# Twelve filler matmuls and a written order in a fused attention and MLP kernel

## The chip, the core and the metric

One core of one Trainium2 chip runs the whole program. The metric is the device time of one execution in microseconds (us); the time of a version is the median over its runs, and lower is better.

## What is computed

Eight batches of attention with eight heads, 576 queries and keys of 64 elements, and 16 beacon keys that every query sees; then a two-layer MLP with a squared ReLU over all 8 x 576 = 4608 tokens.

```python
k_all = np.concatenate([beacon_k, k], axis=2)      # (8, 8, 16 + 576, 64)
v_all = np.concatenate([beacon_v, v], axis=2)
scores = scale * np.matmul(q, k_all.transpose(0, 1, 3, 2))
scores = np.where(causal, -1000000000.0, scores)
a = np.exp(scores - scores.max(-1, keepdims=True))
a /= a.sum(-1, keepdims=True) + 1e-09
attn = np.matmul(a, v_all)                         # -> x: (4608, 512)
...
r = np.maximum(x @ w_in, 0.0)                      # w_in (512, 2048)
out = (r * r) @ w_out                              # w_out (2048, 512)
```

## The kernel before

**Steps.** The kernel is built from 1,521 named steps. A step is an `Op` (L93): a name, the engines that may run it, what it depends on, the buffers that it takes and gives back, and a function that emits its instructions. Names carry the batch or chunk: `ld2k4` loads the fifth slice of batch 2's k (L440), `cast2k4` makes it bf16 on GpSimd (L396), `tr2k` transposes the batch's k by DMA (L472), `qk8.2` computes scores (L687), `exp8.2...` exponentiates them on ScalarE (L789; L711 in batch 0), `mask` applies the causal mask (L811), `av8.0.0` multiplies by v on TensorE (L833), `norm` divides by the row sums (L851, L853), `xt` transposes the result by DMA (L885) into the ring buffer `xT`. Chunks of 512 tokens then go through `s1` (x @ w_in, L1146), `relu` and `sq`, `s2` (the second product, L1197 in the first two chunks, L1260 after them), `ev` (PSUM to `osb`) and `st` (the store to HBM, L1185, L1315).

**Batch 0 and 1** take another way: `fldk`, `fldq`, `sld` load q and k (L586, L515), and TensorE transposes them (`tp`, L547 and L550) into PSUM; `eq` and `ek` copy the result to `qT` and `kT`. In batch 0 the four pairs of heads are computed in two phases (`qk3.0.0`, then `qk3.1.0` and so on). TensorE also transposes the attention output of batches 0 to 2 (`xtp`, L902).

**Queues.** The loads of batches 0 and 1 and both weight matrices are issued by GpSimd (`sld`, `ld0v`, `win`, `sld1`, `ld1v`, `wout`, in this order). All else that is loaded, every DMA transpose and every store but one is issued by SyncE, each in its place in one queue: `ld2k0`, the first of batch 2, waits for the last quarter of `w_out` (`sync`, L1357). Slices pass through six staging buffers `stg`.

**Order.** `Order.run` (L144) is a list planner that runs when the program is built. It keeps a clock of its own with a duration for each step, and whenever an engine is free it starts the ready step of the lowest priority number; `NUDGE` (L17) shifts 275 priorities and `HOME` (L77) binds steps to engines. The steps are emitted in the order of their planned starts. PSUM is handed out as two double banks (`strips`) and four single banks (`ps`); a bank goes back to the end of its list at the moment when the planner's clock sees the step done that reads it last (L181 to L186).

Around the start, TensorE's first work is the transpose `tp0.0.0q`, which waits for `fcq0`, a cast on ScalarE of the first loaded slice of q.

Of the kernel before, what the change touches and what calls it, by code (L numbers as in the profile page):

```python
# [10 lines left out]
BF16 = mybir.dt.bfloat16  # L11
# [5 lines left out]
NUDGE = {  # L17
    "fldk0": 658.071, "fldk1": 538.534, "fcq3": -23.8, "bkl0": 22.188, "ek0.0.0": -25.42, "tp0.0.1k": -476.9,
    "eq0.0.3": -51.138, "tp0.1.0k": -975.238, "eq0.1.0": -201.003, "tp0.1.1k": 92.697, "ek0.1.1": -17.465,
    "tp0.1.2k": -1278.23, "ek0.1.3": -50.758, "eq0.1.3": 210.345, "qk2.1.0": -1322.85, "qk3.1.0": -1576.95,  # L20
    "qk3.1.2": 98696.4, "xte0.0.1": 72.837, "xte0.0.2": 202.007, "xtp0.1.1": 1543.7, "xtp0.1.3": 299.523,
    "tp1.0.0k": -36.734, "tp1.0.2q": 99521.3, "tp1.0.3k": 99518.5, "mask4.0.2": -52.183, "exp5.7.-1.1.0": -4.503,
    "exp5.7.0.0.0": 466.023, "qk6.10": 99505.4, "exp6.10.-1.0.0": 90.776, "exp6.10.-1.1.0": 79.415,
    "exp6.10.1.0.1": 147.224, "exp7.13.-1.1.0": -161.243, "xte1.0.2": 65.923, "s1.0.0.0": -97989.7,
    "relu0.0.0": 0.295, "s1.0.1.0": -98820.7, "relu0.0.1": 179.265, "sq0.0.1": 54.421, "s1.0.2.0": -300.425,
    "s1.0.3.0": -98822.7, "s1.0.2.1": -118.835, "s1.0.3.1": 8.01, "relu0.3.1": -97.929, "sq0.1.1": -91.845,
    "s1.0.8.1": -99593.7, "sq0.4.1": -12.447, "s1.0.11.0": -100291.234, "relu0.10.1": -97.474,
    "s1.0.11.1": -100375.057, "sq0.5.1": -107.919, "sq0.2.0": -108.607, "s1.0.4.1": 45.995, "s1.0.5.1": -257.73,
    "s1.0.6.0": -12.465, "s1.0.7.0": 328.542, "s1.0.6.1": 126.896, "relu0.6.1": 736.189, "s1.0.12.0": -261.69,
    "s1.0.12.1": -260.74, "s1.0.13.1": -30.691, "s1.0.15.0": 310.934, "sq0.7.0": 214.775, "s1.0.14.1": -78.077,  # L30
    "s1.0.15.1": -476.91, "relu0.15.1": 417.533, "s2.0.1.0": 341.138, "s2.0.2.1": 207.549, "s2.0.3.2": 112.672,
    "s1.1.0.0": 108.494, "s1.1.8.0": 54.353, "s1.1.10.0": 53.3, "s1.1.11.0": 94.01, "s1.1.7.0": 463.778,
    "relu1.7.0": 14.618, "s1.1.12.0": 963.577, "ev1.0": -9.252, "st2": 304.472, "s2.1.2.0": 154.455,
    "s2.1.3.2": 256.085, "ev1.3": -16.524, "av8.0.0": 100447.244, "exp9.7.0.0.0": 31.254, "qk10.10": -1291.46,
    "exp10.10.-1.1.0": -214.735, "relu2.0.0": -393.283, "s1.2.1.0": 160.98, "s1.2.8.0": 1108.37, "s1.2.9.0": 1253.63,
    "s1.2.10.0": -101520.500, "relu2.10.0": -9.869, "s1.2.11.0": -99.215, "s1.2.5.0": -101090.066,
    "s1.2.6.0": -100738.217, "s1.2.7.0": -100723.318, "sq2.3.0": -5.02, "s1.2.12.0": -100712.441,
    "s1.2.13.0": -102656.973, "s1.2.14.0": -102349.519, "s1.2.15.0": 239.8, "sum2.4.0": 1465.92, "sum2.3.0": 1466.01,
    "sum2.3.1": 1606.78, "s2.2.1.1": 823.901, "s2.2.5.0": 76.569, "st5": 565.41, "qk12.5": -1133.88,
    "exp12.5.0.0.0": 293.348, "qk13.8": -830.36, "exp14.11.-1.0.0": -65.743, "exp14.11.-1.1.0": 564.369,  # L40
    "mask14.0.1": -1428.96, "norm15.0.0": 218.979, "xt3.1": 8.184, "xt3.3": 202.161, "s1.3.2.0": 16.151,
    "relu3.2.0": 24.317, "s1.3.10.0": -27.427, "s1.3.11.0": 295.381, "s1.3.5.0": 22.355, "sq3.2.0": -7.233,
    "s1.3.7.0": 5.062, "sq3.3.0": 38.235, "s1.3.15.0": 105.093, "sum3.4.0": 2134.7, "s2.3.2.1": -101383.148,
    "s2.3.6.0": -101211.097, "ev3.u2.None": 150.941, "s2.3.4.1": -101244.799, "st7": 333.885, "qk16.2": 101478.821,
    "exp16.5.0.0.0": 448.591, "av18.0.0": 101516.209, "av18.0.1": 101561.876, "av19.0.0": 101281.365, "xt4.0": 2.246,
    "xt4.3": 248.657, "s1.4.0.0": 1038.21, "s1.4.1.0": -912.296, "s1.4.2.0": 57.023, "sq4.1.0": 11.294,
    "s1.4.8.0": 22.523, "s1.4.9.0": -907.487, "s1.4.11.0": 97.493, "sq4.5.0": -5.964, "s1.4.4.0": -101628.248,
    "s1.4.5.0": 124.134, "s1.4.6.0": 259.779, "relu4.7.0": -11.452, "s1.4.12.0": -102373.044, "relu4.12.0": -342.413,
    "sq4.6.0": 2063.88, "s1.4.14.0": -102369.452, "s2.4.2.0": -102160.747, "s2.4.6.0": 1139.26, "s2.4.5.0": 1742.19,
    "ld5k0": -144.81, "ld5k1": 108.018, "ld5v3": -131.083, "exp20.2.1.0.0": 2412.05, "qk20.5": -126.513,  # L50
    "av20.0.1": 601.406, "exp21.8.0.0.0": -36.383, "exp22.11.0.0.0": -3.784, "xt5.2": 229.366, "xt5.3": 136.903,
    "xt5.4": 110.02, "s1.5.0.0": 35.934, "s1.5.1.0": 178.108, "s1.5.2.0": -1138.86, "relu5.2.0": 7.05,
    "s1.5.3.0": 135.127, "sq5.1.0": -15.732, "s1.5.9.0": -1205.53, "s1.5.11.0": -647.533, "s1.5.4.0": 4.138,
    "s1.5.6.0": 127.935, "s1.5.7.0": -102665.329, "relu5.7.0": -5.3, "s1.5.13.0": 1028.46, "sq5.6.0": 95.713,
    "s1.5.15.0": 365.66, "s2.5.6.1": -102540.099, "s2.5.4.1": -102308.653, "ld6q2": 240.402, "tr6k": -117.387,
    "ld6v0": -220.207, "ld6v1": -231.765, "ld6v2": 23.728, "exp24.2.1.0.0": 20.556, "qk24.5": -215.651,
    "exp24.5.-1.0.0": -166.742, "av24.0.0": 102704.684, "av25.0.0": 102763.978, "exp26.11.-1.0.0": 299.914,
    "xt6.1": 154.988, "xt6.3": 265.679, "s1.6.0.0": 1862.08, "s1.6.1.0": 1656.3, "s1.6.2.0": 868.136,
    "relu6.2.0": -22.081, "s1.6.8.0": 10.058, "relu6.8.0": 18.852, "s1.6.9.0": -103734.110, "sq6.4.0": -332.773,
    "s1.6.10.0": -103829.821, "relu6.10.0": 326.623, "s1.6.11.0": -97.927, "relu6.11.0": 31.773, "relu6.4.0": 42.741,  # L60
    "s1.6.6.0": -103698.974, "s1.6.7.0": -581.885, "s1.6.12.0": 60.655, "s1.6.13.0": -41.185, "relu6.13.0": -218.8,
    "relu6.15.0": -324.763, "sum6.4.1": 177.924, "s2.6.7.0": 1165.61, "ev6.u3.None": -28.927, "s2.6.4.1": 2162.64,
    "ld7q4": 33.222, "ld7v2": 112.962, "ld7v4": 152.964, "qk28.5": -420.296, "exp28.5.-1.1.0": 231.981,
    "mask28.0.0": 2691.56, "exp29.8.-1.1.0": 68.674, "exp30.11.-1.0.0": -314.871, "exp30.11.0.0.0": -315.423,
    "exp30.11.0.0.1": -313.054, "qk31.13": 102124.597, "xt7.0": -229.759, "s1.7.0.6": -899.49, "s1.7.0.7": 1016.51,
    "s1.7.0.20": -104119.166, "s1.7.0.50": -66.869, "s1.7.0.30": -832.088, "s1.7.0.21": -958.553,
    "s1.7.0.51": 974.194, "sq7.0.00": 59.755, "relu7.0.10": -5.01, "relu7.0.11": -1.47, "s1.7.1.1": -873.538,
    "s1.7.1.6": -983.885, "s1.7.1.20": -40.299, "s1.7.1.21": 196.468, "relu7.1.01": 109.61, "sq7.1.01": -28.166,
    "sq7.1.11": 55.47, "sum7.1.1": -202.257, "s2.7.2.0": 912.685, "s2.7.5.1": 1296.88, "s2.7.4.0": 1339.65,
    "xsum8.1": 215.859, "s1.8.0.1": -1300.71, "h8.0.c1": -36.926, "h8.0.u2": -108.725, "s1.8.0.4": 900.706,  # L70
    "s1.8.0.20": 10.275, "h8.0.c110": -203.93, "s1.8.0.50": -1927.81, "s1.8.0.21": 365.361, "s1.8.0.51": 135.258,
    "sq8.0.10": 111.703, "s1.8.1.20": -25.178, "h8.1.c110": -94.403, "s1.8.1.50": 20.17, "s1.8.1.21": -0.349,
    "h8.1.c111": -45.509, "s1.8.1.51": -1.323, "sq8.1.00": 27.394, "relu8.1.01": 103.791, "sq8.1.10": -86.019,
    "sq8.1.11": -42.561, "s2.8.1.1": -901.272, "s2.8.7.0": -193.547,
}

HOME = {  # L77
    "fcq3": "ACT", "ek0.0.0": "ACT", "eq0.0.3": "ACT", "eq0.1.0": "ACT", "ek0.1.1": "ACT", "ek0.1.3": "DVE",
    "xte0.0.1": "ACT", "xte0.0.2": "ACT", "xte1.0.2": "DVE", "relu0.0.0": "DVE", "relu0.0.1": "ACT", "sq0.0.1": "ACT",
    "relu0.3.1": "ACT", "sq0.1.1": "ACT", "sq0.4.1": "ACT", "relu0.10.1": "ACT", "sq0.5.1": "ACT", "sq0.2.0": "ACT",  # L80
    "sq0.7.0": "DVE", "relu0.15.1": "ACT", "relu1.11.0": "ACT", "relu1.7.0": "ACT", "ev1.0": "ACT", "ev1.1": "ACT",
    "ev1.3": "ACT", "relu2.0.0": "ACT", "relu2.10.0": "ACT", "sq2.3.0": "DVE", "relu3.2.0": "ACT", "sq3.2.0": "ACT",
# [10 lines left out]
class Op:  # L93
# [6 lines left out]
    def __init__(self, name, engs, dur, emit, prio=0.0, deps=(), take=None, give=None,  # L100
# [11 lines left out]
        self.gate = gate  # L112
        self.held = None
        self.slots = {}
        self.dma = dma
        self.pe_time = pe_time
        self.behind = list(behind)
        self.followers = []


class Order:
# [22 lines left out]
    def run(self):  # L144
# [26 lines left out]
        now = 0.0  # L171
# [1246 lines left out]
```

## Time and profile before

| | |
|---|---|
| three runs | 329.12, 329.96, 331.29 us; median 329.96 |
| span of the profiled execution | 328.4 us (the page gives this execution by its span alone; the median of the runs is 1.56 us above it) |
| busy | TensorE matmuls 313.9 us (96%), VectorE 231.5, ScalarE 225.9, GpSimd 99.9 |
| chain that ended last | TensorE 82%, DMA 10%, VectorE 2%, the rest 6% |
| moved by DMA | 51.98 MB, 158 GB/s over the span |

How to read it: a busy TensorE is not one at its peak, as matmuls are pipelined and their ends modelled. The chain of waits is followed back from the last instruction, at each step to what released it. "SPq" is SyncE's sequencer, which issues DMAs. A DMA share in a window can be above 1, since the times of packets on one engine overlap.

### The profile page before, as it was taken

What the parts mean: (1) busy time and instruction counts of PE and PEld (TensorE: products, weight loads), DVE (VectorE), ACT (ScalarE), POOL (GpSimd) and SP (SyncE); (2) the same over time, 40 slices, a digit from 0 to 9 for tenths busy, and PEclk for the clock granted to TensorE, in tenths of its full rate; (3) what the DMA queues carried; (4) which work ended last, traced back from release to release, by engine and by line L of the source; (5) the groups of instructions that cost most, each with busy time, mean ns of one, the idle gap of its engine ahead of it and who ended that gap; (6) DMA issues with size and microseconds to landing.
All of it is one profiled execution on the core that took longest, in us unless ns stands there. A gap on an engine that the chain in (4) does not pass through costs nothing.

```text
span 328.4 us, 8706 instructions
## 1 busy us (share of the span) xinstructions
PE 313.9 (96%) x3558; PEld 226.7 (69%) x3582; DVE 231.5 (70%) x487; ACT 225.9 (69%) x332; POOL 99.9 (30%) x149
## 2 busy tenths in 40 slices
PE   2999999999999999999989999999989999999995
PEld 1468675544565558888857565776778788888884
DVE  3677885526565899486954788679855797897871
ACT  3877795468775983687576988766837664695931
POOL 9854622503533540425023413542100250000000
PEclk9999999999999999999999999999999999999999
DMA  8999997999999999799999998996913210110033
GB/s 158 219 206 216 203 170 140 213 220 205 207 187 197 245 220 189 139 210 253 186 130 218 231 174 204 214 203 144 211 27 130 46 28 2 66 64 0 2 145 114
DMA packets 145602, 51.98 MB, mean 158 GB/s; under 512 B 132506, under 2 KB 140570, under 8 KB 145562
## 3 DMA queue, kind: packets, MB, share of 16 engines
q1 hardware_dynamic: 135901, 42.32, 64.9%
q0 software_dynamic: 8512, 8.49, 15.3%
q10 hardware_dynamic: 1149, 0.62, 0.8%
q8 instruction: 28, 0.46, 0.6%
q14 instruction: 12, 0.10, 0.1%
HBM read 37.22 MB, written 9.44 MB: 142 GB/s over the span
## 4 chain that ended last, share of the span: by engine, by line
PE 82%; DMA 10%; DVE 2%; SPq 1%; ACT 1%; issue 1%; POOL 1%; POOLq 0%; DVEq 0%
PE ps L1146 25%; PE ps L1260 20%; PE ps L833 8%; PE ps L1197 8%; PE strip L687 6%; PE strip L1020 4%; PE ps L1020 3%; DMA stg<-in_q_dram 2%; PE strip L1260 2%; DMA kT<-qk_area 2%; PE ps L687 2%; PE ps L550 2%; DMA out_dram<-osb 2%; DMA stg<-in_v_dram 1%; PE ps L902 1%; DMA osb<-in_q_dram 1%
## 5 line engine op out<-in xcount | busy, mean ns | idle before, releaser
L1146 PE MATMUL ps<-xT,w_in 128*128 128x512 bf16 (+6 forms) x624 | 105.2, 314 | 2.0 <-DMA xT<-xn 1.2
L1146 PEld LDWEIGHTS <-w_in 128*128 128x128 bf16 x640 | 56.2, 98 | 35.2 <-DMA xT<-xn 1.5
L789 ACT ACTIVATE pt<-strip 128x1024 bf16<-128x1024 f32 (+3 forms) x77 | 69.6, 955 | 7.9 <-PE strip L687 7.7
L1162 ACT ACTIVATE g<-ps 128x512 bf16<-128x512 f32 (+2 forms) x82 | 44.4, 551 | 20.6 <-PE ps L1146 17.7
L396 POOL CAST qk_area<-stg 128x512 bf16<-128x512 f32 (+2 forms) x60 | 40.0, 672 | 54.4 <-DMA stg<-in_k_dram 27.5
L396 POOL CAST vb<-stg 128x512 bf16<-128x512 f32 (+1 forms) x38 | 27.9, 739 | 82.2 <-DMA stg<-in_v_dram 52.8
L811 DVE TENSOR_TENSOR pt<-pt,tri 128x512 bf16<-128x512 bf16 (+1 forms) x93 | 37.7, 423 | 16.0 <-ACT pt L789 14.8
L1260 PEld LDWEIGHTS <-g 128*128 128x128 bf16 x448 | 42.9, 98 | 7.1 <-issue 0.8
L833 PEld LDWEIGHTS <-pt 128*128 128x128 bf16 x930 | 35.1, 99 | 6.9 <-issue 1.2
L1260 PE MATMUL ps<-w_out,g 128*128 128x256 bf16 x304 | 38.0, 273 | 0.0
L833 PE MATMUL ps<-vb,pt 128*128 128x65 bf16 x930 | 37.6, 196 | 0.0
L1164 DVE TENSOR_SCALAR g<-ps 128x512 bf16<-128x512 f32 (+2 forms) x46 | 27.9, 606 | 12.9 <-PE ps L1146 12.5
L1260 PEld LDWEIGHTS <-sum_area 128*128 128x128 bf16 x336 | 32.0, 98 | 6.5 <-issue 2.5
L394 ACT COPY osb<-ps 128x512 f32<-128x512 f32 x26 | 15.2, 586 | 26.4 <-PE ps L1260 19.2
L853 DVE TENSOR_TENSOR xn<-ps,rcp 128x320 bf16<-128x320 f32 (+2 forms) x64 | 31.5, 492 | 2.6 <-DVE rcp L851 0.4
L1174 DVE TENSOR_TENSOR g<-g 128x1024 bf16<-128x1024 bf16 (+2 forms) x35 | 23.7, 682 | 10.3 <-ACT g L1162 9.7
L1197 PE MATMUL ps<-w_out,g 128*128 128x512 bf16 x120 | 30.0, 379 | 0.4
L687 PE MATMUL strip<-qT,kT 64*128 64x128 bf16 (+14 forms) x500 | 29.5, 246 | 0.3 <-ACT qT L394 0.2
L687 PEld LDWEIGHTS <-kT 64*128 64x128 bf16 x618 | 20.0, 95 | 13.9 <-issue 10.2
L1172 ACT ACTIVATE g<-g 128x1024 bf16<-128x1024 bf16 (+2 forms) x29 | 26.8, 942 | 2.6 <-DVE g L1164 1.8
L789 ACT ACTIVATE pt<-ps 128x512 bf16<-128x512 f32 x42 | 23.4, 599 | 5.6 <-PE ps L687 5.0
L1260 PE MATMUL ps<-w_sum,sum_area 128*128 128x256 bf16 x208 | 26.2, 273 | 0.9 <-ACT osb L394 0.9
(91 smaller groups left out, 355.7 us busy)
## 6 DMA issues: line engine op xcount, KB each, us to landing
out_dram<-osb SPq DMA_DIRECT2D x16, 512.0 KB, 3.8
stg<-in_q_dram SPq DMA_DIRECT2D x24, 256.0 KB, 4.7
stg<-in_k_dram SPq DMA_DIRECT2D x18, 256.0 KB, 5.1
stg<-in_v_dram SPq DMA_DIRECT2D x18, 256.0 KB, 4.7
w_in<-in_moe_w_in_dram POOLq DMA_DIRECT2D x4, 512.0 KB, 12.0
w_out<-in_moe_w_out_dram POOLq DMA_DIRECT2D x4, 512.0 KB, 11.3
stg<-in_v_dram POOLq DMA_DIRECT2D x6, 256.0 KB, 8.0
stg<-in_k_dram SPq DMA_DIRECT2D x6, 224.0 KB, 3.7
```

Of the source, the lines that this page charges most:

```text
L396: eng[e].tensor_copy(dst, src)
L687: nc.tensor.matmul(out, kT[b % 2][hp, pr, 128 * c:128 * c + 128], rhs, start=True, stop=True)
L789: nc.scalar.activation(out, in_, AF.Exp, bias=0.0, scale=scale)
L811: nc.vector.tensor_tensor(out=d, in0=d, in1=tri[0:rows, m0:m0 + m, 0:w][:, None].to_broadcast([rows, 2, m, w]), op=ALU.min)
L833: nc.tensor.matmul(a[:, at + (t - tl[0]) * (D + 1):at + (t - tl[0] + 1) * (D + 1)], P[0:rr, hj, o:o + 128], vb[b % 2][0:rr, c, 2 * pr + hj ...
L853: nc.vector.tensor_tensor(out=xn[b % 2].rearrange("p t (h d) -> p h t d", d=D)[:, h0:h0 + nh, tl[0]:tl[0] + nt], in0=a[:, :, :, 0:D], in1= ...
L1146: nc.tensor.matmul(h[:, lo - spans[0][0]:hi - spans[0][0]], w_in_sb[:, mc, ft * 128:(ft + 1) * 128], xT[:, mc, lo % RING:lo % RING + hi - lo],
L1162: nc.scalar.activation(dst, h, AF.Relu, bias=0.0, scale=1.0)
L1164: nc.vector.tensor_scalar(out=dst, in0=h, scalar1=0.0, scalar2=None, op0=ALU.max)
L1172: nc.scalar.activation(d, d, AF.Square, bias=0.0, scale=1.0)
L1197: nc.tensor.matmul(o, G[:, fc, ts * 128:(ts + 1) * 128], w_out_sb[:, fc, :], start=(fc == 0), stop=(fc == NFT - 1))
L1260: nc.tensor.matmul(o, lhs[:, f, t * 128:(t + 1) * 128], rhs[:, f], start=fresh and f == 0, stop=f == HF - 1, skip_group_check=True)
```

## The change

The planner, its priorities, `NUDGE`, `HOME`, the limits on PSUM use and the pacing of attention against the MLP are taken out. In their place stands the order as a text: 1,525 words, each a step's name and, where two engines may run it, a letter for the engine. `Order.run` walks the words and emits.

Against the order that the planner of the kernel before makes, the 1,521 old steps stand in the same sequence, on the same engines. Four steps are new, on TensorE: `fill0` ahead of everything, `fill1` behind `tp0.0.0q`, `fill2` behind `tp0.0.3k`, `fill3` behind `tp0.0.2q`. They multiply a zeroed part of `g[0]` by itself into one half of a strip, and nothing reads the result. The zeroing is a new memset, the first instruction of VectorE.

One thing differs without a step of its own: a bank goes back to its list when the step that reads it last is emitted, not when a planner's clock sees it done. So banks are handed out in another sequence: 204 of the steps that take `ps` banks get another number, and for 38 of them the step that held the bank before is another one.

```diff
+SEQUENCE = """
+fill0 ident tri fldq0 fldk2 fldq1 bkl0 fldq2 fldk1 warm sld0k1.0 fldk0 sld0q1.0 fcq0 sld0k1.2 tp0.0.0q fill1 eq0.0.0@D
+sld0q1.2 fck2 tpg0.0.0q fck3 tp0.0.2k fcq1 ld0v0 bkc0 tp0.0.3k fill2 ek0.0.2@A ek0.0.3@D tpg0.0.2k tpb0 tpg0.0.3k
+tp0.0.1q ekb0 fcq3@A fcq2@D ld0v1 bkl1 eq0.0.1@A tp0.0.3q fck1 tpg0.0.1q tp0.0.2q fill3 ld0v2 eq0.0.3@A eq0.0.2@D
...
     def run(self):
...
+        named = {op.name: op for op in self.ops}
+        self.issued = []
+        for word in SEQUENCE.split():
+            name, _, letter = word.partition("@")
+            op = named.pop(name)
+            e = self.LETTER[letter] if letter else op.engs[0]
+            assert e in op.engs and all(d.done for d in op.need + op.behind), name
+            for pool, need in op.take:
+                op.slots[pool] = [self.pools[pool].pop(0) for _ in range(need)]
+                op.held = op.held or (pool, op.slots[pool][0])
+            op.done = True
+            self.issued.append((op, e))
             if e != "-":
                 op.insts = op.emit(e)
...
+            for given in op.give:
+                from_op, which, pool = (*given, None)[:3] if isinstance(given, tuple) else (given, 0, None)
+                pool = pool or from_op.take[0][0]
+                self.pools[pool].append(from_op.slots[pool][which])
...
+    nc.vector.memset(g[0][:, 0, :], 0.0)
     nc.vector.memset(warm, 0.0)
...
+    FILLS = {"fill0": [512] * 9, "fill1": [512], "fill2": [256], "fill3": [256]}
...
+    def add_fill(name, widths):
+        def emit(e):
+            for w in widths:
+                nc.tensor.matmul(strips[fill.held[1]][:, 0, 0:w], g[0][:, 0, 0:128], g[0][:, 0, 0:w], start=True, stop=True)
+
+        fill = add(name, "PE", sum(widths) / 1200.0, emit, take=("strip", 1))
+        fill.give = [fill]
```

## The prediction

> **What bounds the kernel now.** First the page's busy times and slices: TensorE is busy 96% of the span, but the DMA engines are as full as they get until about slice 29 of 40 (238 us), so both have to be followed.
>
> ```profile
> PE 313.9 (96%) x3558; PEld 226.7 (69%) x3582; DVE 231.5 (70%) x487; ACT 225.9 (69%) x332; POOL 99.9 (30%) x149
> ...
> DMA  8999997999999999799999998996913210110033
> ```
>
> Second the timeline of the first 33 us, for the stage that is changed.
>
> ```profile
> 0.93 0.14 DVE L375 MEMSET kT<- 128x96 uint32 x1
> ...
> 5.51 0.38 PE L547 MATMUL ps<-ident,qk_area 120*128 120x120 bf16 x2 [5.51 <-ACT qk_area L394]
> ...
> 14.03 0.69 POOL L515 DMA_DIRECT2D qk_area<-in_k_dram  x1
> 15.91 0.84 PE L833 MATMUL ps<-vb,pt 128*128 128x65 bf16 x12
> 21.67 2.12 PE L833 MATMUL ps<-vb,pt 128*128 128x65 bf16 x48
> 31.89 0.45 PE L550 MATMUL ps<-ident,qk_area 96*64 96x96 bf16 x12
> ```
>
> TensorE has nothing to do until 5.51. The same matmul of 65 columns then costs (0.84 - 0.25 for the last to drain) / 11 = 54 ns at 15.9, while the chain has 24 of them in 0.73 us at 26.09, 30 ns each; the 48 at 21.67 take 2.12 us, between 48 x 54 = 2.6 and 48 x 30 = 1.4, so the clock rises inside that row, near 22.8. The clock column prints 1.00 for the opening too, so it is read from durations here. TensorE runs at about half clock from 5.5 to 22.8, 17 us.
>
> Third, what that costs the engine that computes beside it (waits of ScalarE from 9 to 24):
>
> ```profile
> ACT pt L711 <- PE strip L687: 1.7, 3, 0.7
> ACT xT L394 <- PE ps L902: 0.8, 1, 0.8
> ACT sum_area L711 <- PE strip L687: 0.8, 2, 0.6
> ```
>
> 3.3 us of idle ScalarE there wait for TensorE. Fourth, how far a gain at 24 us can travel. The waits of SyncE's queue, its timeline around 62 us, and the waits of TensorE from 160 to 240:
>
> ```profile
> SPq L439 <- DMA w_out<-in_moe_w_out_dram: 47.0, 1, 47.0
> ```
>
> ```profile
> 57.91 1.93 SPq L440 DMA_DIRECT2D stg<-in_k_dram  x2
> 62.14 0.39 SPq L1185 DMA_DIRECT2D out_dram<-osb  x1
> 62.62 0.42 SPq L440 DMA_DIRECT2D stg<-in_k_dram  x1
> 63.13 5.26 SPq L472 DMA_TRANSPOSE qT<-qk_area  x1
> ```
>
> ```profile
> PE ps L1146 <- DMA xT<-xn: 1.2, 1, 1.2
> PE ps L1260 <- ACT osb L394: 0.9, 1, 0.9
> PE ps L687 <- DMA kT<-qk_area: 0.4, 1, 0.4
> ```
>
> SyncE's loads for batch 2 to 7 begin at 50.35, when the last quarter of w_out has landed (50.14), and from there to 235 the queue issues almost without a pause. TensorE catches up with it three times: at 170.6 it waits 1.2 us for `xt4.0`; at 224.84, 0.4 us for `tr7k`; at 240.4 `av28.0.0` starts 0.1 us behind the cast of `ld7v4`, which landed at 239.52. The end of the program hangs on when SyncE's queue is through, plus 88 us of work behind that, not on when TensorE began.
>
> **The change, part by part.**
>
> *The memset* is VectorE's first instruction, 512 bf16 = 256 words. At the row above, 0.14 us for 96 words, it costs at most 0.37 us, ends near 1.25, and VectorE's next real work is at 5.93: nothing.
>
> *fill0.* At full clock 512 columns take 1.73 / 8 = 216 ns (chain, L1197, 55.43); at half clock 0.43. Nine take 3.9 us, 1.3 to 5.2, and about 0.2 to drain. `tp0.0.0q` can start at 5.51 because a cast ends then, so the fill fits by a tenth or two. If weight loads (98 ns each) were not hidden, it would end at 6.1 and delay the first transpose by 0.6; in the rows of L1146 and L1197 they are hidden, so I take zero.
>
> *Does it raise the clock, and does the clock stay?* The trace has one rise, after some 3.4 us in which score and attention matmuls followed each other closely; 3.9 us of back-to-back columns are denser than that. For staying, the sparsest stretch at full clock is around 169, with the 1.2 us wait: there matmuls stream half of 3.4 us. Between 5.5 and 8.9 the changed kernel streams fill1 to fill3 (1,024 columns, 0.43 us) and twelve transposes of 120 columns (0.6 us): 30%, and 13% by matmuls alone. No row shows either outcome; two in three for staying, as the gaps are all below 1 us. [...]
>
> *fill1 to fill3* sit in waits: TensorE is idle 0.62 us before 6.52, 0.39 before 7.48, 0.25 before 8.87; they cost 0.21, 0.11, 0.11 (twice that at half clock). Zero; without that cover at most 0.86.
>
> *The early gain.* At full clock, half of the 3.3 us that ScalarE waits goes: 1.6; ends: 0 (clock falls back) and 3.6 (all of it, and 0.3 for the first scores). I take 1.6, as the waits contain fixed drains too. It is capped: the first transpose of batch 1 (31.89) needs the load issued at 14.03. Its view gives 15.6 us to landing, so 29.65, and this GpSimd queue moves 205 to 215 GB/s without a gap whatever TensorE does. More than 2.2 us of lead cannot pass there. Behind it `av4.0.0` has 2.2 us to its last cast of v and `s2` 3 us to the last quarter of w_out, so 1.6 reaches 60 us.
>
> *What the lead does to SyncE's queue.* One place before 235 has it idle for TensorE's sake: 59.84 to 62.14, waiting for `ev0.3` to store the first half chunk. A lead of 1.6 issues that store and `ld2k4` at 60.5. Next is `tr2q`, which waits for a cast ending at 61.26 + 1.65 = 62.91, so the issue moves by 0.2 only. But store and slice (2.5 + 0.8 us of transfers) then fill the dip that follows: the DMA share from 62 to 66 is 0.96, against 1.36 in the 4 us before it and 1.27 in the 4 us behind. 4 x (1 - 0.96 / 1.2) = 0.8 us of transfers find room. The queue gains between 0.2 and 0.8 us; I take 0.5. No later store or transpose finds it idle: each one's producer is done before the instruction ahead is issued, or the wait is for a cast behind a load. So 0.5 us arrives at `tr7k` and at the end; the other 1.1 are waited out at 170.6 and 224.84.
>
> *The banks.* Set against the trace of before, the new predecessor of a bank finishes too late in four of the 38 places: `tp1.0.0q` (0.13 us), `s1.0.15.0` (0.3), `s1.2.9.0` (0.3), `s1.4.13.0` (0.4, at 185.15). 1.1 us in all, every one before 186, where the waits at 170.6 and 224.84 cover them: zero. Without that cover, 1.1. No other instruction moves: every engine's and every queue's order is the old one.
>
> *Sum.* 328.4 - 0.5 = 327.9 us of span; the median of the runs stood 1.56 above it: 329.4.
>
> **The rivals.**
>
> A, *the lead survives* (12%): SyncE's queue is not rigid, DMA transposes get shorter when the transfers ahead of them leave earlier (`tr2q` issues for 5.3 us, later ones for 3.1 to 4). For it: the chain enters the queue at 194 from TensorE's side through VectorE. Against: three catch-ups with no slack. Price: up to the cap, 329.96 - 2.2 = 327.8.
>
> [...]
>
> C, *slower* (12%): the bank swap takes the cover's place. `s1.4.13.0` waits 0.4 us for a relu on VectorE at 185; with TensorE holding only 0.4 at 224.84, any second stall past 170.6 of more than 0.1 us makes `qk28.5` and all behind it late, and the releases of PSUM slip further as they follow each other. It decides once stalls after 170.6 exceed 0.4 in sum; with all 1.1 us uncovered, 331.1.
>
> The forecast itself has 46%.
>
> **How the numbers follow.** 329.4 is the likeliest. The range runs from A's end with 0.4 for the scatter (327.4) to C's end with the same (331.5); three runs of one kernel differ by 2.2 us. 1% (3.3 us, about what a measurement can tell here) is crossed by none of the cases: faster needs below 326.66, more than the cap lets through, slower above 333.26. I leave 8% for faster and 7% for slower, for shifts of DMA timing that I have not seen; 85% within 1%.
>
> **What would show it.** [...] The early gain: the first `s1` at 22 to 23 instead of 24.3, the first transpose of batch 1 not before 29.7. The hiding: TensorE's wait for `xT` near 170 grows from 1.2 by the lead, and `tr7k` lands between 224.0 and 224.6. I am wrong if `tr7k` lands before 223.5 or after 225.5, or if SyncE's queue shows TensorE as the releaser between 70 and 235.

## The result and the profile after

The changed kernel took 332.54 us (median of 13 runs, 330.83 to 333.85) against 330.41 us for the kernel before in the same comparison (13 runs, 327.96 to 332.71): a ratio of 1.0057, 95% interval 1.0035 to 1.0079. It is slower by about half a per cent, where 329.4 was forecast and the range ended at 331.5. All ratios in this document leave out executions that took over 1.5% longer than the fastest of their kernel (at most two of a kernel), while medians are of all executions. The profiled execution took 330.92 us, with a span of 329.2.

The page of the changed kernel: its busy times, two rows of slices, and one DMA queue (beside its name: packets, MB, and the packets' time as a share of 16 engines' span):

```profile
PE 318.4 (97%) x3570; PEld 228.6 (69%) x3594; DVE 231.8 (70%) x488; ACT 225.6 (69%) x332; POOL 100.2 (30%) x149
...
PEclk9659999999999999999999999999999999999999
DMA  8999999998999999999969998999913210110033
...
q8 instruction: 28, 0.46, 0.6%
```

TensorE has 12 more matmuls and 4.5 us more busy time, about what the fills take. The clock row now shows two dim slices (8 to 25 us), and the DMA engines are still full until about 238 us. The line on queue 8 stood in the page of before too, and the prediction did not read it; it comes back below.

The timeline of the changed kernel's opening (`fill0`, the first transpose, `fill1`, `fill2`), and its rows for the attention matmuls of 65 columns that the prediction read in the kernel before:

```profile
0.94 0.27 DVE L319 MEMSET g<- 128x256 uint32 x1 [0.94 <-PEq L1325]
...
1.26 4.02 PE L524 MATMUL strip<-g 128*128 128x512 bf16 x9 [1.26 <-DVE warm L320]
...
5.41 0.38 PE L493 MATMUL ps<-ident,qk_area 120*128 120x120 bf16 x2
...
5.58 0.63 PE L524 MATMUL strip<-g 128*128 128x512 bf16 x1
...
6.69 0.28 PE L524 MATMUL strip<-g 128*128 128x256 bf16 x1
```

```profile
15.32 0.84 PE L772 MATMUL ps<-vb,pt 128*128 128x65 bf16 x12
...
21.08 2.73 PE L772 MATMUL ps<-vb,pt 128*128 128x65 bf16 x48
```

The memset and `fill0` lie where they were expected, and the first transpose starts at 5.41 instead of 5.51. `fill1` still runs at half clock (512 columns in 0.63 us; the prediction reckoned 0.43 of streaming at half clock and 0.2 of drain); `fill2` does not (256 columns in 0.28, where half clock would give about 0.41 by the same reckoning). At 15.3 the 12 matmuls of 65 columns take 0.84 us, exactly as before: half clock again. And the 48 at 21.08 now take 2.73 us instead of 2.12, so that the lasting rise comes later than before. The granted clock in the trace says when: up at 6.51, down at 9.92, up for good at 23.57; before it rose once, at 22.79. The windows of the changed kernel (start and end in us; length; busy time and instructions of PE, PEld, DVE, ACT and POOL; clock, DMA share, GB/s):

```profile
5.50:9.90 4.40, 3.55 (x35) 1.60 (x35) 3.85 (x12) 2.57 (x6) 4.38 (x6) 1.00 1.49 202
9.90:22.80 12.90, 12.84 (x162) 7.79 (x161) 9.44 (x30) 11.05 (x18) 9.43 (x15) 0.50 1.20 215
22.80:50.00 27.20, 27.15 (x407) 20.77 (x407) 22.02 (x53) 21.63 (x41) 11.45 (x18) 0.99 1.11 192
```

So the early gain did not come. ScalarE's waits from 9 to 24 us in the changed kernel add up to 3.6 us in these rows, where they were 3.3:

```profile
ACT pt L654 <- PE strip L632: 1.4, 3, 0.7
ACT xT L341 <- PE ps L840: 1.4, 1, 1.4
ACT sum_area L654 <- PE strip L632: 0.8, 2, 0.6
```

A small lead (0.58 us at 21) was gone when TensorE entered the MLP. How the two traces then stand against each other, in us (TensorE's starts are those of the first weight load, up to 0.1 us before the matmul):

| | before | after | difference |
|---|---|---|---|
| TensorE starts `av0.1.0` | 21.66 | 21.08 | -0.58 |
| TensorE starts `s1.0.1.0` | 24.26 | 24.29 | +0.03 |
| SyncE issues `ld2k0` | 50.35 | 49.39 | -0.96 |
| TensorE starts `qk20.2` | 164.38 | 164.48 | +0.10 |
| `st1` has landed | 67.76 | 65.95 | -1.81 |
| `tr3k` has landed | 99.83 | 100.43 | +0.60 |
| `tr5k` has landed | 160.69 | 161.86 | +1.17 |
| `xt4.0` has landed | 170.61 | 171.92 | +1.31 |
| TensorE starts `s1.4.12.0` | 170.65 | 171.96 | +1.31 |
| `tr7k` has landed | 224.80 | 226.20 | +1.40 |
| TensorE starts the last `s2` | 323.46 | 324.32 | +0.86 |

For 140 us TensorE runs 0.1 us behind the old times and no more. SyncE's queue even begins ahead of the old times, and the landing of `st1` still is. The loss appears in that queue between 75 and 170 us, in steps of which some are partly won back, and TensorE learns of it where it catches up with the queue. Its waits from 160 to 240 us in the changed kernel:

```profile
PE ps L1074 <- DMA xT<-xn: 2.4, 1, 2.4
PE ps L632 <- DMA kT<-qk_area: 0.4, 1, 0.4
```

The chain of waits of the changed kernel passes through the queue at that place (start, us, what):

```profile
168.15 0.46 PE strip L632 x10
168.61 0.84 SPq L823
169.49 2.42 DMA xT<-xn
172.41 1.46 PE ps L1074 x6
```

This transpose itself takes as long as before (2.44 then, 2.42 now). What is late is its issue. So two things have to be explained: a clock that fell back, and a queue of loads that runs slower although all its instructions stand in the old order.

### The profile page after: what moved, and what is told of

It is laid out like the page before. It is cut to its first block, busy times and chain, and to the rows that moved or that the text cites. A ratio compares the mean times of both kernels' runs of the same rounds, so it can differ in the third digit from the quotient of the medians.

```text
span 329.2 us, 8733 instructions
## 1 busy us (share of the span) xinstructions
PE 318.4 (97%) x3570; PEld 228.6 (69%) x3594; DVE 231.8 (70%) x488; ACT 225.6 (69%) x332; POOL 100.2 (30%) x149
## 3 DMA queue, kind: packets, MB, share of 16 engines
q0 software_dynamic: 8512, 8.49, 15.3%
## 4 chain that ended last, share of the span: by engine, by line
PE 82%; DMA 10%; SPq 3%; DVE 2%; ACT 1%; issue 1%; POOL 1%; ACTq 0%; DVEq 0%; POOLq 0%
PE ps L1074 25%; PE ps L1183 20%; PE ps L772 8%; PE ps L1124 8%; PE strip L632 6%; PE strip L951 4%; PE ps L951 3%; DMA stg<-in_q_dram 2%; PE strip L1183 2%; DMA kT<-qk_area 2%; PE ps L632 2%; DMA osb<-in_q_dram 2%; PE ps L496 2%; DMA out_dram<-osb 1%; PE ps L840 1%; DMA stg<-in_k_dram 1%
## 5 line engine op out<-in xcount | busy, mean ns | idle before, releaser
L343 POOL CAST vb<-stg 128x512 bf16<-128x512 f32 (+1 forms) x38 | 26.4, 704 | 86.0 <-DMA stg<-in_v_dram 85.5
L1101 DVE TENSOR_TENSOR g<-g 128x1024 bf16<-128x1024 bf16 (+2 forms) x35 | 24.4, 705 | 10.7 <-ACT g L1089 10.1
```

The source lines that it names most:

```text
L343: eng[e].tensor_copy(dst, src)
```

## The experiments

Each ratio is to the kernel before on the same chip, with its 95% interval; 9 to 12 executions stand against 29 to 35 of the kernel before. The executions of one kernel scatter by some 5 us (the kernel before: 327.23 to 332.41 on one chip), so one trace can show a mechanism but not half a per cent.

**Banks or fills.** Four kernels: the written order without fills and memset, with the planner's bank numbers (all as before) or the new ones; the fills with the planner's numbers; the whole change again.

```diff
 # without fills: the four words and the memset go
-fill0 ident tri fldq0 ...
+ident tri fldq0 ...
-    nc.vector.memset(g[0][:, 0, :], 0.0)
 # the planner's bank numbers, read from a list
-                op.slots[pool] = [self.pools[pool].pop(0) for _ in range(need)]
+                if pool == "ps":
+                    op.slots[pool] = [int(c) for c in next(banks)]
+                else:
+                    op.slots[pool] = [self.pools[pool].pop(0) for _ in range(need)]
```

Expected of the old banks without fills:

> The written order with the banks of before and without fills: instruction for instruction the program of before, so a control. Every theory expects a ratio of 1.000 to the kernel before; how far it strays (I allow 0.3%, 1 us) says what a difference between two equal programs looks like here.

Of the new banks without fills:

> The written order with the changed handing out of PSUM banks, no memset and no fills. Theory banks: this alone is slower by the whole 1.9 us (ratio 1.004 to 1.008). Theory fills: no change (ratio 0.998 to 1.002), clock rising near 22.8 as before. Theory scatter (the DMA queue's timing differs by a few us from run to run and nothing is systematic): ratio 0.998 to 1.002.

Of the old banks with fills:

> The memset and the twelve fills with the banks of before. Theory banks: no change (ratio 0.998 to 1.002). Theory fills: slower by the whole 1.9 us (1.004 to 1.008), the clock rising at 5 to 7 us and falling back near 10. Theory scatter: 0.998 to 1.002.

Of the whole change:

> The changed kernel once more, beside its parts on one chip. Theories banks and fills: ratio 1.004 to 1.008 again. Theory scatter: nearer to 1.000, below 1.003.

Measured, in this order: 1.0003 (0.9976 to 1.003), 0.9992 (0.9972 to 1.0012), 1.0074 (1.0041 to 1.0106), 1.0055 (1.0022 to 1.0088). Neither the banks nor the text in place of the planner cost anything that shows. The fills carry the loss.

**The clock.** All 12 fills with 16 columns each; `fill0` alone; and larger fills (the late ones twice as wide) with 42 more of 256 columns behind TensorE's steps up to 25 us, to hold the clock.

```diff
-    FILLS = {"fill0": [512] * 9, "fill1": [512], "fill2": [256], "fill3": [256]}
+    FILLS = {"fill0": [16] * 9, "fill1": [16], "fill2": [16], "fill3": [16]}      # light
...
+    FILLS = {"fill0": [512] * 9}                                                  # fill0 alone
...
+    FILLS = {"fill0": [512] * 9, "fill1": [512, 512], "fill2": [512], "fill3": [512],
+             "fill4": [256], "fill5": [256],
...
```

Expected of the light fills:

> All twelve fills and the memset, but 16 columns each in place of 512 and 256, so the same instructions with a thirtieth of the columns. Theory clock (the fills raise TensorE's clock once, it falls back, and this excursion is what costs): clock stays low until 22 to 25 us as before, ratio 0.998 to 1.002. Theory instructions (the memset, twelve more instructions and their waits on TensorE cost by themselves): ratio 1.004 to 1.008.

Of `fill0` alone:

> The memset and fill0 alone, fill1 to fill3 taken out. Theory clock: the clock still rises between 4.8 and 6.5 us and falls back one window later; ratio 1.004 to 1.008. Rival, that the three late fills cost, not the first: ratio 0.998 to 1.002.

Of the held clock:

> The changed kernel with a further fill of 256 columns behind each of 42 early steps of TensorE up to 24 us, and 512 in fill1 to fill3, so that the clock should stay up from 5 to 24 us. If the falling back is what costs: with the clock held the ratio is below 1.002, and 0.993 if TensorE's lead of 2 us survived to the end. If what costs is TensorE being ahead of, or out of step with, the loads: ratio 1.004 or more although the clock never falls.

Measured: light 1.0027 (0.9996 to 1.0059), with one rise of the clock at 23.68; `fill0` alone 0.9987 (0.9958 to 1.0016), although its clock too was up from 6.11 to 9.53 and down until 23.18; held 1.0044 (1.0015 to 1.0074). Its windows:

```profile
0.00:4.00 4.00, 2.74 (x7) 1.04 (x8) 0.66 (x6) 1.49 (x2) 3.25 (x13) 1.00 0.38 106
4.00:9.90 5.90, 4.91 (x44) 2.09 (x41) 3.26 (x11) 2.72 (x7) 5.87 (x9) 1.00 1.41 206
9.90:22.70 12.80, 12.80 (x175) 7.19 (x170) 9.51 (x30) 10.43 (x16) 9.01 (x13) 1.00 1.19 217
```

The clock stays up from 4.01 us to the end (the changed kernel has 0.50 in the third row), and the kernel is as slow as with the clock that falls. It had no lead either, since the added matmuls eat it: `av0.0.0` starts at 16.64, before at 15.90. So this run does not price a lead; it shows that the loss comes without the falling back as well. The light fills point the same way, with a doubtful interval.

**Which fills.** `fill1` to `fill3` alone; all 12 with the late three at 16 columns; 12 matmuls all ahead of the first transpose; the whole change a third time.

```diff
-fill0 ident tri fldq0 ...
+ident tri fldq0 ...                                                              # late fills alone
...
+    FILLS = {"fill0": [512] * 9, "fill1": [16], "fill2": [16], "fill3": [16]}     # late ones light
...
+    FILLS = {"fill0": [512] * 8 + [128] * 4}                                      # twelve first
```

Expected of the late fills alone:

> The zeroed tile and fill1 to fill3 alone, without the nine matmuls ahead of the first transpose; the clock should rise once, near 23 us, as before. Theory 'columns of the late fills' (1,024 columns between the early transposes set the early order of work back, and the loss comes out in the queue of loads): ratio to the kernel before 1.004 to 1.007, about that of the whole change (1.0055). Theory 'mere presence of the late fills': the same. Theory 'number of added instructions' (12 in the whole change, 3 here): 1.000 to 1.002. Theory 'together only' (the late fills cost because they run in the short stretch at the raised clock, or because of what that stretch does): 0.998 to 1.002.

Of the light late fills:

> The whole change, but fill1 to fill3 of 16 columns each; fill0 keeps its nine of 512. Theory 'columns of the late fills': 0.998 to 1.001, as with fill0 alone (0.9987). Theory 'mere presence': 1.004 to 1.007. Theory 'number of added instructions': 1.004 to 1.007, since all 12 are there. Theory 'together only': 0.998 to 1.002.

Of the twelve ahead:

> Twelve fills as in the whole change, all of them ahead of the first transpose (eight of 512 columns and four of 128, so that the columns are those of fill0), none behind it. Theories 'columns of the late fills' and 'mere presence': 0.997 to 1.001. Theory 'number of added instructions': 1.004 to 1.007. Theory 'together only': 0.997 to 1.001.

Of the whole change:

> The whole change unaltered, on the same chip as its three parts, for the comparison: 1.004 to 1.008 by every theory that takes the two ratios measured so far (1.0057 and 1.0055) for the change's own; 1.000 to 1.002 if they were chance. In its profile the clock should be up for one window of 3.4 us after the fills and down again until about 23 us.

Measured: 1.0004 (0.9975 to 1.0032), 1.0030 (1.0001 to 1.0059), 1.0033 (1.0003 to 1.0063), 1.0012 (0.9979 to 1.0046). The last one misses the ratio expected; its median over all twelve executions stood 0.58% above that of the kernel before. Weighted by their intervals, the three ratios of the whole change give 1.0046. The late fills are not the cause, neither by columns nor by presence, since without them 12 matmuls ahead cost about as much. What was left: the number of added matmuls, or that nine alone had been a lucky sample.

**Number, columns and place.** `fill0` alone again; 12 and 60 matmuls of 16 columns ahead of the first transpose; 12 behind TensorE's last matmul.

```diff
+    FILLS = {"fill0": [16] * 12}           # twelve light first; [16] * 60 for sixty
...
 # twelve light last: the word moves to the end
-s2.8.3.1 ev8.c21.1@A
+s2.8.3.1 fill0 ev8.c21.1@A
```

Expected of `fill0` alone, again:

> The nine matmuls alone once more (zeroed tile and fill0 of nine times 512 columns, no late fills). Theory 'number of added matmuls, from twelve up': 0.997 to 1.001, as the first time. Theory 'every kernel with fill0, the first sample was lucky': 1.003 to 1.007.

Of the twelve light ones:

> Twelve fills of 16 columns each, all ahead of the first transpose, none behind it; the clock should rise once, near 23 us. Theory 'number of added matmuls': 1.004 to 1.007. Theory 'fill0's columns, and with them the short stretch at the raised clock': 0.999 to 1.001.

Of the sixty:

> Sixty fills of 16 columns ahead of the first transpose. Theory 'number of added matmuls': 1.004 or more, up to five times the cost of twelve if it grows with the number (1.02 and over), 1.004 to 1.007 if it is a step. Theory 'fill0's columns and the short stretch at the raised clock': 0.999 to 1.001, unless these sixty raise the clock too.

Of the twelve at the end:

> Twelve fills of 16 columns behind TensorE's very last matmul of the program, none ahead. Theory 'number of added matmuls, by the length of the program': 1.004 to 1.007. Theory 'number of added matmuls, by where they push the instructions behind them': 0.999 to 1.002, since only the last two stores stand behind them. Theory 'columns': 0.999 to 1.002.

Measured: 1.0032 (0.9995 to 1.0068), 1.0034 (1.0002 to 1.0066), 1.0056 (1.0024 to 1.0088), 1.0011 (0.9990 to 1.0032). The nine alone thus stand at 0.9987 once and 1.0032 once, and their case stays undecided. Columns are out: the sixty light ones are done 1.8 us after they begin, the clock does not move before 23 us, and they cost as much as the whole change. Sixty do not cost five times what twelve cost, so it is no price per matmul. At the end of the program the twelve cost next to nothing.

Here the line of queue 8 came in: 28 packets of 16 KB, 0.46 MB in all. TensorE's stream without fills has 7,164 instructions (3,582 matmuls and 3,582 weight loads in the page of the old banks without fills; the trace of the kernel before lacks 24 of its matmul records). That is about 256 for each packet, and in the traces one such packet begins for every 250 or so of TensorE's recorded instructions. No other engine has more than 600 on record. The count alone does not settle it, since the changed kernel has 24 instructions more and still 28 packets. The reading is that the blocks are TensorE's instructions, brought in by the 16 DMA engines, whose time the page of the kernel before divides between queue 8 (0.6%) and the queues of the data (64.9, 15.3 and 0.8%). Every matmul brings its weight load along (3,582 of each, and with the fills the page has 12 more of each): twelve fills push the rest of the stream by 24 instructions, and each later block is fetched 24 instructions earlier in the work. Three runs were made for this: one matmul ahead (a push of 2, TensorE still starts early), 128 ahead (a push of 256, a whole block, so the fetches come at the old places again), and twelve behind `s1.0.10.0`, which ran at 30.3 us where about 27 was expected (a push of 24 without an early start).

```diff
+    FILLS = {"fill0": [16]}                # one; [16] * 128 for a whole block
...
 # twelve in the middle: the word moves, with [16] * 12
-s1.0.10.0 relu0.9.0@A
+s1.0.10.0 fill0 relu0.9.0@A
```

Expected of the one:

> The zeroed tile and one matmul of 16 columns ahead of the first transpose, nothing else. Theory 'early start of TensorE': 1.003 to 1.006. Theory 'place in the stream of instructions': 0.999 to 1.002. Theory 'number of added matmuls': 0.999 to 1.002.

Of the 128:

> 128 matmuls of 16 columns ahead of the first transpose: 256 instructions, one whole block of the stream, done by about 5 us. Theory 'place in the stream of instructions': 0.999 to 1.002, as the later blocks are fetched at the same places of the work as before. Theories 'early start' and 'number of added matmuls': 1.003 to 1.007.

Of the twelve in the middle:

> Twelve matmuls of 16 columns at about 27 us, behind s1.0.10.0, none ahead of the first transpose; TensorE's lead there shrinks by some 0.4 us. Theory 'place in the stream of instructions': 1.003 to 1.006. Theory 'early start': 0.999 to 1.002. Theory 'number of added matmuls': 1.003 to 1.006.

Measured: 0.9987 (0.9962 to 1.0013), 1.0001 (0.9976 to 1.0025), 1.0040 (1.0011 to 1.0069). All three fall as "place in the stream of instructions" said (the first just below its band). "Early start" wanted 1.003 and more of the first two, above both intervals, and "number" wanted it of the 128. The page of the kernel before and that of the kernel with 128 differ by the one extra block:

```profile
q8 instruction: 28, 0.46, 0.6%
...
q8 instruction: 29, 0.48, 0.6%
```

Some of the times at which the blocks are fetched (trace, us; the blocks are counted as in the kernel before):

| kernel | extra block | 1st | 2nd | 6th | 14th | 20th |
|---|---|---|---|---|---|---|
| before | | 19.2 | 27.6 | 65.8 | 156.2 | 222.8 |
| 128 ahead | 7.1 | 19.5 | 28.0 | 67.4 | 157.5 | 223.8 |
| whole change | | 17.3 | 26.1 | 62.8 | 154.6 | 222.3 |
| sixty ahead | | 12.0 | 24.2 | 57.1 | 148.9 | 219.8 |

These times also carry each trace's own lag. Set against TensorE's own work, that is, against the time at which the kernel before reaches the same weight load, the fifteen fetches between 52 and 240 us come earlier on average by 0.1 us with 128 ahead and by 0.1 to 0.2 with a push of 0 to 6. With 18 they come 0.9 and 1.1 us earlier, with 24 by 1.0 to 1.3, with 110 and 120 by 5.1 and 6.0.

All runs, ordered by the push:

| push, instructions | kernels | ratios |
|---|---|---|
| 0 up to the last matmul | control, new banks, twelve at the end | 1.0003, 0.9992, 1.0011 |
| 2 and 6 | one ahead, late fills alone | 0.9987, 1.0004 |
| 18 | `fill0` alone, twice | 0.9987, 1.0032 |
| 24 | whole change, three times | 1.0057, 1.0055, 1.0012 |
| 24 | the five others with twelve fills ahead or early, and twelve in the middle | 1.0074, 1.0027, 1.0030, 1.0033, 1.0034, 1.0040 |
| 110 and 120 | held clock, sixty ahead | 1.0044, 1.0056 |
| 256 | 128 ahead | 1.0001 |

From 24 to 120 the eleven ratios have a mean of 1.0042; the six at 0 to 6 and 256 have 1.0000. That a whole block brings the old time back rests on one kernel.

**What a fetch does to a transpose.** The DMA view of 153 to 159 us (40 slices of 0.15 us), first of the kernel before:

```profile
GB/s 218 273 410 382 423 423 410 437 255 287 288 295 287 290 292 290 290 288 288 295 287 384 275 246 7 0 58 10 7 10 10 9 51 282 290 244 239 294 285 294
...
q8 instruction: 1, 0.02, 1.0%
```

then of the changed kernel:

```profile
GB/s 285 314 218 218 437 423 341 423 437 382 388 270 270 227 2 0 0 3 7 9 10 10 20 275 292 288 294 288 285 297 285 292 292 288 275 265 259 229 220 220
...
q8 instruction: 1, 0.02, 1.1%
```

In each the one fetch (1.0% and 1.1% of 16 engines x 6 us; the traces have 0.95 us of one engine before and 1.06 after) is followed by a hole of eight or nine slices, 1.2 to 1.35 us, in which hardly anything moves, with transposes in flight. The hole begins at 156.6 before and at 155.1 after. SyncE's timeline shows what it lands on. Kernel before, `tr5q` and `tr5k` (start, us in which SyncE is held by the issue):

```profile
151.40 4.22 SPq L472 DMA_TRANSPOSE qT<-qk_area  x1
155.71 3.74 SPq L472 DMA_TRANSPOSE kT<-qk_area  x1
```

Changed kernel:

```profile
151.65 5.14 SPq L420 DMA_TRANSPOSE qT<-qk_area  x1
156.88 3.12 SPq L420 DMA_TRANSPOSE kT<-qk_area  x1
```

Sixty ahead, where no fetch falls into this stretch and the longest dip is of two slices:

```profile
GB/s 270 375 372 401 372 374 387 314 205 232 188 183 205 236 220 166 212 246 225 218 218 218 217 218 217 217 217 218 217 218 212 178 45 118 229 219 208 203 224 227
...
153.26 3.41 SPq L420 DMA_TRANSPOSE qT<-qk_area  x1
156.76 3.17 SPq L420 DMA_TRANSPOSE kT<-qk_area  x1
```

The other traces show it too. In the 19 besides that of the twelve at the end, between 52 and 235 us, 186 fetches lie wholly between a transpose's issue and its landing, and 125 of them are followed, within 0.9 us of the packet's end, by a hole (under 60 GB/s for 0.8 us or more, up to 1.7). Of the 114 other fetches, 5 are. But holes come without a fetch too: 69 of 199.

`tr5q` holds the queue for 3.41 us without a fetch, 3.8 to 4.2 in the traces where one comes 3.6 to 5.2 us behind its issue, and 5.1 in the six where it comes at 2.2 to 3.0. `tr7q` lands 4.9 to 5.2 us behind its issue in the traces without a fetch inside it, and 6.2 to 6.8 in the five with one, and there `tr7k`, right behind it, holds SyncE for 3.6 to 3.9 us, where it does for 3.1 to 3.2 in most others. So in these places a fetch inside a DMA transpose goes with a landing that is later by 1.0 to 1.9 us (`tr7q`), and with 0.4 to 1.7 us more in which SyncE's queue is held (`tr5q`; 0.4 to 0.8 at `tr7k`). One trace does not fit: with the held clock `tr5q` holds the queue for 4.9 us, though its fetch begins 0.7 us before the issue and none inside.

How one packet of 16 KB, recorded as 0.95 or 1.06 us of one engine, comes to hold up the others is not shown by any run. That they stand still as well is seen only in the traces above.

**What stays open.** Which of these collisions make the 0.4%. They do not simply add up: a fetch falls into 20 of the 37 transposes in the trace of before and into 18 in that of the changed kernel, and what the fetches add between issue and landing is not larger there. What differs is where in a transpose they come: from 100 us on, SyncE is held by transposes for 66.0 to 67.1 us (mean 66.5) in six traces (the kernel before, both without fills, late fills alone, one and 128 ahead), and for 66.5 to 70.9 (mean 68.4) in the eleven at 24 to 120; `fill0` alone has 66.9 and 67.3. That fits a loss of 1 to 2 us, but the two ranges overlap, with one trace of each kernel. So the place of the fetches is shown as the cause by the ratios, and the way from there to the loss, through the transposes, is argued. Why the old places should be the better ones, and why a shift of 6 us costs no more than one of 1 us, is not shown. Nor was it tried to move the fetches with anything but matmuls.

## Why the prediction failed, step by step

*Memset, `fill0`, first transpose* (nothing, ends at 1.25, 5.51): right within 0.1 us, with 0.27 us ending at 1.21, and 5.41.

*"Two in three for staying"*: wrong. The prediction set the 30% of streaming in 5.5 to 8.9 beside the half that it had found around 169, and took gaps below 1 us for the better sign; that was its author's estimate. The clock fell back after 3.41 us (after twice that in one of the other traces), although TensorE's rows fill 3.55 of the 4.40 us from 5.50 to 9.90, and the twelve matmuls of 65 columns took 0.84 us again, 54 ns each as before. The traces agree on the length: up for 3.41 us, then down for 13.65 here and 17.07 in the kernel with old banks and fills, which are four and five times 3.413. By the rows, the stretch in which it fell was no idle one, and what made it fall is not shown. Nor do the "some 3.4 us" of close matmuls show what makes it rise: in the kernel before, TensorE is busy for 3.41 of 3.41 us up to the rise at 22.79, but for 3.40 of 3.40 from 15.90 as well. The forecast (46%) and the rivals A and C (12% each) left 30% for a clock that falls back.

*"The early gain", 1.6 us, and 0.5 of it through the queue*: both zero, as the clock was down from 9.9 to 23.6. The store that was to move from 62.14 to 60.5 was issued at 62.24. The 0.5 was not tested; it rested on a dip in the DMA share from 62 to 66, where the same windows show no dip in bytes (243 and 201 GB/s, after 222 and 198). With these terms the sum is 327.9 + 1.56 = 329.46, so 329.5 and not 329.4.

*The banks, "zero"*: right (0.9992). TensorE's lag on the old times grows by about 0.16 us where nothing of the queue delays it (0.08 by 50 us, 0.08 near 186), against 1.1 for the stalls; rival C fell.

*"Zero" for the fills, and "no other instruction moves"*: this is the step that made the time wrong. As columns on TensorE the fills are indeed free: TensorE is at its old times within 0.1 us from 25 to 165. The order of every queue is the old one. But 24 instructions ahead of 7,164 move the places where instruction blocks are fetched, and with the clock back down the whole change did not run at the old time but at 1.0046 of it (three ratios by weight). In place of the zero the runs showed a price of 0.42% on the mean for a push of 24 to 120 instructions, and none for a push of a whole block. The rows for it were in the page: 28 packets on queue 8, beside transposes in a queue without slack.

*"The end of the program hangs on when SyncE's queue is through"*, and leads "are waited out at 170.6 and 224.84": right, and it worked the other way round. TensorE's wait at 170.6 grew from 1.2 to 2.4 as foreseen, but because `xt4.0` landed 1.31 us later and not because TensorE was early; and `tr7k` landed at 226.20, past the 225.5 that the prediction had named as its refutation.

*The bounds*: the range covered a gain and covered stalls on TensorE, but had no term for a slower queue. The 7% for slower by over 1% were meant for "shifts of DMA timing"; the size was half of that, in the gap that was left between 331.5 and 333.3.

No version here beats the kernel before: without the fills the written order runs the same time (0.9992), and no fill gave a measurable gain.

## What to carry to other kernels

An instruction that costs nothing where it stands still lengthens its engine's stream: here twelve matmuls of 16 columns ran at a ratio of 1.0034 ahead of the work and of 1.0011 behind it. Where the DMA queue has no slack, count the instruction fetches in the queue table and ask where a shift puts them. Test such a suspicion by padding with light instructions, up to a whole block, which brought the old time back here (1.0001). And before paying for a pre-warmed clock, look for the first queue that the engine's lead catches up with; what a lead is worth there no run here priced, as the one of 0.58 us at 21 us was gone at 24.3.

## What the runs showed of the hardware

Queue 8 has 28 packets of 16 KB for TensorE's 7,164 instructions and 29 with 256 more, about 256 to a packet; read as TensorE's instructions, they take 0.88 to 1.56 us each in the traces of the kernel before and the changed one, and the page gives them 0.6% of the time of the 16 DMA engines, beside the data's queues. Behind such a packet DMA transposes in flight often stood still: in 125 of 186 cases, for 0.8 to 1.7 us.

The recorded changes of the granted clock lie 3.413 us or whole multiples of it apart: 3.413 and 13.653 in the changed kernel, 17.07 with the old banks and fills. With the wide matmuls back to back from 1.26 it rose at 4.01 (held clock), 6.11 (`fill0` alone) and 6.51 (the whole change), with light ones in their place at 23.68, and in the kernel before at 22.79. What TensorE does from 5.5 to 9.9 (busy 3.55 of 4.40 us) did not hold it beyond one or two steps of 3.413 us, and in the stretch that follows, with transposes, scores and attention in turn (busy 12.84 of 12.90 us), it came back only after four or five. What it takes to raise or to hold it is not shown.

The clock column reads 1.00 for a time at which matmuls run at half speed if no change has been recorded yet: before has 1.00 from 9.9 to 22.8 in the window view, where twelve matmuls of 65 columns take 0.84 us, and the changed kernel has 0.50 there with the same 0.84. Until the first recorded change, the clock is read from durations.
